# Two linear-attention blocks on one core: M's products spread over four token pairs, kv's products in two runs of three, and q's first loads given due times

## The chip, the core and the metric

The kernel runs on one core of a Trainium2 chip. The metric is the device time of one execution in microseconds. The core's engines work in parallel, each through its own queue in order: TensorE (PE; its weight loads are listed as PEld), VectorE (DVE), ScalarE (ACT), GpSimd (POOL) and SyncE (SP), which here only issues DMA transfers. An instruction that waits for a semaphore holds up everything behind it in its engine's queue.

## The reference

Two independent blocks, A and B, with inputs of their own; their results stand side by side. S = 2048 tokens, D = 640, 32 heads of 20.

```python
qkv = (x @ wqkv).reshape(B, S, 3, H, Dh)          # q, k, v
phi = lambda t: where(t > 0, t + 1, exp(t)) + 1e-6
pq, pk = phi(q), phi(k)
kv  = einsum("bhsd,bhse->bhde", pk, v)
z   = einsum("bhsd->bhd", pk)
num = einsum("bhqd,bhde->bhqe", pq, kv)
den = einsum("bhqd,bhd->bhq", pq, z) + 1e-6
return (num / den) @ wo                            # per block
```

## The kernel before, in words

All arithmetic is float32 made of pairs: a value is split into a high part (ACT rounds it, `hi_of`) and a low part (DVE subtracts, `lo_of`), and a product takes three matmuls. The value side is never formed per token. Instead G = x^T phi(k) is summed over tokens (`gstep`, tile psg, sums kept in gacc), kv = wv^T G per group of heads (`kvmm`, tile pskv, six groups of 6, 6, 6, 6, 4 and 4 heads, masked to the blocks of the heads), and M = kv wo (`mmm`, tile psm evacuated to mev, six groups too). M goes to memory (`md`), comes back (tile m), is turned into the nine sums that a Strassen-like product needs and into high and low parts (`forms("m", ...)` within `m_forms`), and those go to memory once more (fdh, fdl), from where the output stage loads them (fh, fl).

The first part of the kernel, some 290 us, handles k for both blocks. Tokens go through in pairs of tiles (`kpair(p, fill)`, 8 pairs a block, NPB = 8, NP = 16; pairs 0 to 2 take another path). A pair has seven steps of products (banks 0, 1 and 2 as tiles ka, ke, kb), each followed by evacuations on ACT and DVE (`copy`, `plus`) and by what `fill` puts there: gsteps of the group before, kv's products, M's products. Pairs 8 to 15 belong to block B; in them block A's kv and M are made. After pair 15 ten gsteps of the last group remain, and then the second part begins: the q stage, whose order is written out by hand (`at(slot, ...)`): products psq over 512 tokens, block B's own kv and M, the denominators and the output products (pa, pe, psb).

Order within the first part comes from a planner, run on the host while the program is built. Each job has an engine, an estimated cost, what it reads and writes, and optionally `ahead` (it may not be placed earlier than so many us before it is due), `late` (the due time of a job that nobody in the plan waits for, counted from `pe_at`, the sum of PE's costs so far, 25 by default), `due` (a fixed due time) and `safe` (a margin after a transfer). Due times are computed backwards from the readers. `emit` then walks forward in its own clock: each engine takes, of its jobs that are ready, the one due first, if tiles for it are free. A transfer costs wire time at 330 KB/us and is believed to have landed 1.9 us after that; its buffers are free from then on. PE's order is that of the calls. The chip then runs these orders against real semaphores.

Tiles come from slots: GD (31 of 640 columns), BD (7) and BO (4) are shared by nearly everything. The pool kx (for pairs) is closed by a planned job `gate`, and q1a and q1b (for q) open in its place. q's first loads are planned too: five pieces of wq (split into wh, wl), five of x (xqs, rounded to xqh), five low parts of x from memory (xql) and block B's wv.

z, the sum of phi(k) over tokens, is accumulated by transfers of GpSimd (`z_add`, zacc) and finished by `zsums`: DVE sums, transposes and reduces (zp), a store to memory (zd), four small loads (zq) and four small DVE steps (z, zs).

Of the kernel before, what the change touches and what calls it, by code (L numbers as in the profile page):

```python
# [15 lines left out]
DH = 20  # L16
EPS = 1e-6
GROUPS = [(0, 6), (6, 6), (12, 6), (18, 6), (24, 4), (28, 4)]
LAG = 0.2


class Space:
# [53 lines left out]
class Plan:  # L76
# [6 lines left out]
        self.jobs = []  # L83
        self.pe_at = 0.0

    def note(self, engine, n, fn, w, r, ahead=None, dma=None, late=None, by=None, due=None, safe=0.0):
# [22 lines left out]
        j.by, j.set, j.safe = by, due, safe  # L109
        self.jobs.append(j)  # L110
        return j

    def emit(self, start, log=None):
        jobs = self.jobs
        for j in reversed(jobs):
            due = min([n.due - LAG for n in j.nexts], default=j.late)
            if j.by is not None:
                due = min(due, j.late)
            due -= j.cost + (2.2 + j.dma if j.dma else 0)
            if j.engine == "PE":  # L120
                due = min(due, j.ideal)
            j.due = due if j.set is None else j.set
# [14 lines left out]
        while n < len(jobs):  # L137
# [7 lines left out]
            for e in idle:  # L145
# [46 lines left out]
                queue[e].remove(best)  # L192
                if best.dma:
                    wire = max(wire, now) + best.dma
                    best.done = wire + 1.9
                    if e == "SP":
                        flying.append(best.done)
                    idle[e] = now + best.cost
                else:
                    best.done = idle[e] = now + best.cost  # L200
                events.update((idle[e], best.done, best.done + LAG))
                ends.append((best.done, best))
                best.fn()
                if log is not None:
                    log.append((now, e, best.fn.__code__.co_firstlineno, best, best.done))
# [10 lines left out]
def tile_linear_attn_pair(ctx: ExitStack, tc: tile.TileContext, ins, out: bass.AP):  # L216
# [79 lines left out]

    BK = [Bank("bank", k) for k in range(8)]

    def load(dst, src, n, ahead=14.0, due=None):
        note("SP", 0.07, lambda: nc.sync.dma_start(dst.f, src), [dst], [], ahead=ahead, dma=n * 512 / 330e3, due=due)  # L300

    def hi_of(hi, src, n):
        note("ACT", n, lambda: act(hi.r, src.f, AF.Copy), [hi], [src], ahead=10.0)
# [51 lines left out]
    def forms(kind, src, split, ready=()):  # L355

        f, raw = {}, {}
        for c in range(NC):
            raw[c] = t = Space(kind, D, ANY)
            note("SP", 0.07, lambda t=t, c=c: nc.sync.dma_start(t.all.f, src[c * P:(c + 1) * P, :]), [t.all],  # L360
                 [mdv[0:6]] if kind == "m" else [], ahead=14.0, dma=1.0)
        for k in range(2):
            m, n = raw[k], raw[2 + k]
            x, z = Space("t23", D, ANY), Space("t4", HF, ANY)
            note("DVE", HF, lambda m=m, n=n, x=x: tt(x[HF:D].f, n[HF:D].f, m[HF:D].f, op=OP.subtract),
                 [x[HF:D]], [n[HF:D], m[HF:D]], ahead=10.0)
            note("DVE", HF, lambda m=m: tt(m[HF:D].f, m[HF:D].f, m[0:HF].f, op=OP.subtract),
                 [m[HF:D]], [m.all], ahead=10.0)
            note("DVE", HF, lambda m=m, n=n, x=x: tt(x[0:HF].f, n[HF:D].f, m[HF:D].f, op=OP.subtract),
                 [x[0:HF]], [n[HF:D], m[HF:D]], ahead=10.0)  # L370
            note("DVE", HF, lambda n=n, x=x, z=z: tt(z.all.f, n[0:HF].f, x[0:HF].f, op=OP.subtract),
                 [z.all], [n[0:HF], x[0:HF]], ahead=10.0)
            f[k], f[2 + k], f[4 + k], f[6 + k] = m, x, n, z
        x, m = Space("d5", HF, ANY), raw[4]
        note("DVE", HF, lambda: tt(x.all.f, m[0:HF].f, m[HF:D].f, op=OP.subtract), [x.all], [m.all], ahead=10.0)
# [211 lines left out]
    def zsums(b):  # L587

        z, zt32 = Space("zsum", D, ANY), Space("zturn", D, ANY)
        for h in range(2):  # L590
            note("DVE", HF, lambda h=h: tt(z.all.f[:, h * HF:h * HF + HF], zac[b][h].all.f[:, :HF],
                                           zac[b][h].all.f[:, HF:], op=OP.add), [z[h * HF:h * HF + HF]], [zac[b][h].all], safe=6.0)
        part, four = Space("zpart", 20), Space("zfour", 20)
        pt, ft4 = zp[b]
        add = dict(axis=mybir.AxisListType.X, op=OP.add)
        note("DVE", D, lambda: nc.vector.transpose(zt32.all.f, z.all.f), [zt32.all], [z.all])
        note("DVE", D, lambda: nc.vector.tensor_reduce(
            pt.rearrange("p (g c) -> p c g", g=4), zt32.all.f.rearrange("p (c g t) -> p c g t", g=4, t=32), **add),
            [part.all], [zt32.all])
        zdv = Space("zd", 1)  # L600
        note("SP", 0.07, lambda: nc.sync.dma_start(zd[b], pt), [zdv.all], [part.all], dma=0.1)
        for g in range(4):
            note("SP", 0.07, lambda g=g: nc.sync.dma_start(
                ft4[g * 32:g * 32 + 32].rearrange("p (q c) -> p q c", q=4),
                zd[b].rearrange("(q i) (g c) -> g i q c", q=4, g=4)[g]), [four[g:g + 1]], [zdv.all], dma=0.1, safe=6.0)
        zt, s = zz[b]

        def finish():
            nc.vector.tensor_reduce(zt, ft4.rearrange("p (q c) -> p c q", q=4), **add)
# [8 lines left out]
    def m_forms():  # L618
        def split(i, s):
            hi = Space("fsh", s.cols, ANY, F32R)  # L620
            lo = Space("fsl", s.cols, ANY, F32R)
            hi_of(hi.all, s.all, s.cols)
            lo_of(lo.all, s.all, hi.all, s.cols)
            fd[0, i] = [dram.tile([P, s.cols], F32, name=f"fd{t}0{i}") for t in "hl"]
            for d, t in zip(fd[0, i], (hi, lo)):
                note("SP", 0.07, lambda d=d, t=t: nc.sync.dma_start(d, t.all.f), [], [t.all], dma=s.cols / 640,
                     late=16.0 + 8.0 * (0, 2, 6, 4, 1, 3, 7, 5, 8, 9).index(i))

        forms("m", md[0], split)

# [161 lines left out]
    for c in range(NC):  # L792
        gstep(NG - 1, 0, c)
    wf[1] = forms("wk", ins[1]["wk"], w_split)
    kpair(NPB, filled(NG - 1, 1))
    kpair(NPB + 1, {0: [(kvmm, 0, 6)], 1: [(kvmm, 1, 7)], 2: [(kvmm, 2, 6)], 3: [(kvmm, 3, 7)],
                    4: [(kvmm, 4, 6), (kvmm, 5, 7)], 5: [(mmm, 0, 6)], 6: [(mmm, 1, 6)]})
    for p in range(NPB + 2, NP):
        i, h = divmod(p - NPB - 2, 2)
        gready(NG + i)  # L800
        fl = filled(NG + i, h, *((LAST,) if p == NP - 1 else ()))
        if p == NPB + 2:
            for n, g in ((0, 2), (2, 3), (4, 4), (6, 5)):
                fl.setdefault(n, []).append((mmm, g, 6))
        kpair(p, fl)
        if p == NPB + 2:
            zsums(0)
            m_forms()

    def swap():  # L810
# [28 lines left out]
    for c in range(NC):  # L839
# [8 lines left out]
            lo.make()  # L848
            tt(lo.all.r, raw.all.f, hi.all.f, op=OP.subtract)

        note("ACT", D, high, [hi.all], [raw.all, gate.all])
        note("DVE", D, low, [lo.all], [raw.all, hi.all])
        whl["q", 0, c] = hi, lo
    for c in range(NC):
        hi, lo, raw = late(q1b, "xqh", 512, 6), late(q1b, "xql", 512, 6), Space("xqs", 512, ANY)
# [7 lines left out]
            lo.make()  # L863
            nc.sync.dma_start(lo.all.f, xd[0][:, c].rearrange("p j s -> p (j s)"))

        note("ACT", 512, round, [hi.all], [raw.all, gate.all])
        note("SP", 0.07, fetch, [lo.all], [gate.all, xdv[0].all], ahead=30.0, dma=0.8)
        xt[0, c] = hi, lo
    for g, (h0, nh) in enumerate(GROUPS):
        cols = NC * DH * nh  # L870
        w = Space("wv", cols, (BD,))
        load(w.all, ins[1]["wv"][:, h0 * DH * NC:(h0 + nh) * DH * NC], cols, 30.0)
        w.left += 1
        wvt[1, g] = w
    plan.emit(1.0, globals().get("LOG"))
# [515 lines left out]
```

## Time and profile before

| | |
|---|---|
| median of 3 runs | 572.95 us (572.63 to 574.16) |
| profiled execution | 574.53 us, span 572.8 us from first to last instruction |
| PE busy | 565.7 us of the span |
| DVE, ACT, POOL busy | 434.3, 341.4, 57.2 us |
| granted clock of PE | 0.999 |
| DMA | 117.64 MB, mean 205 GB/s |
| chain that ended last | PE 89%, DMA 5%, DVE 3% |

A row of the order of time reads: start and duration in us, engine, line, operation, output and inputs, tile sizes, how many were merged (x), and in brackets how long the engine stood idle before it and what ended that. Matmuls are pipelined, so one lasts 0.31 us by its row while the next starts 0.15 us after it. A row of the waits reads: who waited, for whom, us in total, times, the longest. In the table by stages each stretch has its length, then busy time with the number of instructions for PE, PEld, DVE, ACT and POOL, the granted clock, the DMA share and GB/s. A row of transfers reads: out and in, queue, count, KB each, median us from issue to landing.

### The profile page before, as it was taken

What the parts mean: (1) busy time and instruction counts of PE and PEld (TensorE: products, weight loads), DVE (VectorE), ACT (ScalarE), POOL (GpSimd) and SP (SyncE); (2) the same over time, 40 slices, a digit from 0 to 9 for tenths busy, and PEclk for the clock granted to TensorE, in tenths of its full rate; (3) what the DMA queues carried; (4) which work ended last, traced back from release to release, by engine and by line L of the source; (5) the groups of instructions that cost most, each with busy time, mean ns of one, the idle gap of its engine ahead of it and who ended that gap; (6) DMA issues with size and microseconds to landing.
All of it is one profiled execution on the core that took longest, in us unless ns stands there. A gap on an engine that the chain in (4) does not pass through costs nothing.

```text
span 572.8 us, 9505 instructions
## 1 busy us (share of the span) xinstructions
PE 565.7 (99%) x3524; PEld 535.8 (94%) x3524; DVE 434.3 (76%) x706; ACT 341.4 (60%) x619; POOL 57.2 (10%) x93
## 2 busy tenths in 40 slices
PE   8999999999999999999999999999999999999997
PEld 6999999999999999999988899898989989898997
DVE  6788687599888589976555699967788786758792
ACT  6877566673786677655156665646556464644551
POOL 0210011110010011100000103120012201001010
PEclk9999999999999999999999999999999999999999
DMA  8994665758858889786787986663363996122022
GB/s 296 379 242 141 163 183 128 205 143 246 278 144 217 250 249 321 216 252 196 211 245 275 339 276 215 226 218 109 120 225 134 355 390 231 47 76 93 0 93 92
DMA packets 69441, 117.64 MB, mean 205 GB/s; under 512 B 7956, under 2 KB 31252, under 8 KB 69396
## 3 DMA queue, kind: packets, MB, share of 16 engines
q1 hardware_dynamic: 60500, 89.98, 48.2%
q0 software_dynamic: 8608, 26.88, 16.7%
q8 instruction: 27, 0.44, 0.3%
q10 hardware_dynamic: 288, 0.20, 0.1%
q14 instruction: 18, 0.15, 0.1%
HBM read 71.13 MB, written 35.41 MB: 186 GB/s over the span
## 4 chain that ended last, share of the span: by engine, by line
PE 89%; DMA 5%; DVE 3%; ACT 1%; issue 1%; SPq 1%; ACTq 0%; DVEq 0%
PE psg L312 20%; PE pa L1191 12%; PE ka L312 8%; PE psq L912 8%; PE psq L914 8%; PE psq L913 8%; PE pe L1191 6%; PE ke L312 4%; PE psk L711 4%; PE psb L1191 4%; PE kb L312 3%; DMA md<-mev 2%; DMA wk<-in_A_wk 1%; PE pskv L551 1%; PE pskv L972 1%; DMA xqs<-in_A_xt 1%
## 5 line engine op out<-in xcount | busy, mean ns | idle before, releaser
L312 PE MATMUL psg<-pkl,xnh 128*128 128x320 f32 x320 | 98.9, 309 | 0.0
L312 PE MATMUL psg<-pkh,xnh 128*128 128x320 f32 x320 | 98.8, 309 | 0.0
L312 PE MATMUL psg<-pkh,xnl 128*128 128x320 f32 x320 | 98.4, 308 | 0.0
L912 PE MATMUL psq<-xqh,wh 128*128 128x512 f32 x200 | 78.6, 393 | 1.0 <-ACT xqh L860 1.0
L914 PE MATMUL psq<-xqh,wl 128*128 128x512 f32 x200 | 78.0, 390 | 0.0
L913 PE MATMUL psq<-xql,wh 128*128 128x512 f32 x200 | 77.9, 390 | 0.0
L312 PEld LDWEIGHTS psg<-pkl,xnh 128*128 128x128 f32 x320 | 60.1, 188 | 0.0
L312 PEld LDWEIGHTS psg<-pkh,xnl 128*128 128x128 f32 x320 | 60.1, 188 | 0.0
L312 PEld LDWEIGHTS psg<-pkh,xnh 128*128 128x128 f32 x320 | 60.0, 188 | 0.0
L1206 ACT ACTIVATE o<-pa 128x320 f32<-128x320 f32 x64 | 27.9, 438 | 45.2 <-PE pa L1191 45.0
L484 ACT ACTIVATE kt<-ka 128x320 f32<-128x320 f32 x52 | 22.6, 435 | 52.2 <-PE ka L312 49.0
L1082 DVE SCALAR_TENSOR_TENSOR pq<-eq,rq 128x512 f32<-128x512 f32 x40 | 27.6, 691 | 30.7 <-ACT rq L1081 30.6
L401 POOL DMA_DIRECT2D zacc<-ek x32 | 26.4, 836 | 244.5 <-DVE ek L494 185.3
L532 DVE TENSOR_TENSOR gacc<-psg,gacc 128x320 f32<-128x320 f32 x60 | 29.4, 489 | 28.1 <-PE psg L312 27.3
L1080 ACT ACTIVATE eq<-psq 128x512 f32<-128x512 f32 x40 | 23.9, 597 | 36.6 <-PE psq L914 34.2
L912 PEld LDWEIGHTS psq<-xqh,wh 128*128 128x128 f32 x200 | 37.6, 188 | 8.5 <-ACT xqh L860 1.3
L914 PEld LDWEIGHTS psq<-xqh,wl 128*128 128x128 f32 x200 | 37.5, 188 | 7.9
L913 PEld LDWEIGHTS psq<-xql,wh 128*128 128x128 f32 x200 | 37.6, 188 | 7.2
L396 ACT ACTIVATE pkh<-ek,epst 128x640 fp32r<-128x640 f32 x32 | 26.5, 829 | 7.9 <-DVE ek L494 7.5
L1191 PE MATMUL pa<-fh,dah 128*128 128x320 f32 x96 | 29.7, 309 | 0.0
L1191 PE MATMUL pa<-fh,dal 128*128 128x320 f32 x96 | 29.7, 309 | 0.0
L1191 PE MATMUL pa<-fl,dah 128*128 128x320 f32 x96 | 29.7, 309 | 0.0
(213 smaller groups left out, 1553.3 us busy)
## 6 DMA issues: line engine op xcount, KB each, us to landing
zacc<-ek POOLq DMA_DIRECT2D x32, 320.0 KB, 5.8
xql<-xd SPq DMA_DIRECT2D x40, 256.0 KB, 5.9
xd<-xl SPq DMA_DIRECT2D x29, 320.0 KB, 6.2
out<-o POOLq DMA_DIRECT2D x28, 320.0 KB, 3.6
xns<-in_A_x SPq DMA_DIRECT2D x16, 320.0 KB, 5.8
xts<-in_B_xt_tiles SPq DMA_DIRECT2D x16, 320.0 KB, 4.3
xns<-in_B_x SPq DMA_DIRECT2D x16, 320.0 KB, 5.1
xqs<-in_A_xt SPq DMA_DIRECT2D x20, 256.0 KB, 6.0
```

Of the source, the lines that this page charges most:

```text
L312: nc.tensor.matmul(o, a.r, w.r, start=start and k == i == 0, stop=k == n - 1 and i == 2, skip_group_check=True)
L396: note("ACT", n + 110, lambda: act(hi.r, p.f, AF.Identity, bias=epst), [hi], [p, K0.all], by=8.0)
L401: note("POOL", 1.0, lambda: nc.gpsimd.dma_start(z.f, p.f, **kw), [z], [p], dma=1.0 if first else 1.86)
L532: tt(o, BK[k].tile[:, :HF], o, op=OP.add)
L711: nc.tensor.matmul(o[h][:, :HF], x[a].r, w[c][h * HF:h * HF + HF].r, start=c == 0 and i == 0, stop=c == NC - 1 and i == 2, skip_group_chec ...
L912: nc.tensor.matmul(o, whi, xhi, start=first, stop=False)
L913: nc.tensor.matmul(o, whi, xlo, start=False, stop=False)
L914: nc.tensor.matmul(o, wlo, xhi, start=False, stop=last)
L1080: nc.scalar.activation(e, ps, AF.Exp)
L1082: nc.vector.scalar_tensor_tensor(pq[u][:, c, :], e, 1.0, r, op0=OP.min, op1=OP.add)
L1191: nc.tensor.matmul(ps, x, y, start=start and n == i == 0, stop=n == len(terms) - 1 and i == 2, skip_group_check=True)
L1206: copy = lambda x, y: nc.scalar.activation(x, y, AF.Copy)
```

## The change

1. The planner: a transfer is believed to have landed `lat` after the wire, 3.0 us (LAT) instead of 1.9, unless it has a fixed due time; a transfer's buffers count as taken for 6 us (REUSE) after that. Due times of transfers move earlier by the same 1.1 us.
2. kv's products of block A, one after each of steps 0 to 3 and two after step 4 of pair 9, become two runs of three, after steps 1 and 4.
3. M's products: two in pair 9 and four in pair 10 become one in pair 9 (step 5), two in pair 10 (steps 0 and 2), two in pair 11 (steps 0 and 2), one in pair 12 (step 0). Pair 10's gsteps take the later places (LAST).
4. `zsums(0)` follows pair 12 and `m_forms()` pair 13; both followed pair 10. The stores of M's forms get closer due times, and the differences of M's rows a margin (`safe`) of 6 us.
5. The z store and its four loads are issued by GpSimd instead of SyncE, for both blocks.
6. q's first jobs get due times of their own: splits of wq 9 us after the end of PE's planned work instead of 25, rounding of x 8, low parts of x 6 to 10, wv 10 to 20; `ahead` is smaller for the low parts and wv.

```diff
+LAT = 3.0
+REUSE = 6.0
 ...
+        j.by, j.set, j.safe, j.lat = by, due, safe, (LAT if due is None else 1.9) + lat
 ...
-            due -= j.cost + (2.2 + j.dma if j.dma else 0)
+            due -= j.cost + (j.lat + 0.3 + j.dma if j.dma else 0)
 ...
-                    best.done = wire + 1.9
+                    best.done = wire + best.lat
 ...
-                events.update((idle[e], best.done, best.done + LAG))
-                ends.append((best.done, best))
+                free = best.done + (REUSE if best.dma else 0.0)
+                events.update((idle[e], best.done, best.done + LAG, free))
+                ends.append((free, best))
 ...
     def forms(kind, src, split, ready=()):
+        safe = 6.0 if kind == "m" else 0.0
 ...
-        note("SP", 0.07, lambda: nc.sync.dma_start(zd[b], pt), [zdv.all], [part.all], dma=0.1)
+        note("POOL", 1.0, lambda: nc.gpsimd.dma_start(zd[b], pt), [zdv.all], [part.all], dma=0.1, lat=2.0)
         for g in range(4):
-            note("SP", 0.07, lambda g=g: nc.sync.dma_start(
+            note("POOL", 1.0, lambda g=g: nc.gpsimd.dma_start(
 ...
-                     late=16.0 + 8.0 * (0, 2, 6, 4, 1, 3, 7, 5, 8, 9).index(i))
+                     late=10.0 + 5.5 * (0, 2, 6, 4, 1, 3, 7, 5, 8, 9).index(i))
 ...
-    kpair(NPB + 1, {0: [(kvmm, 0, 6)], 1: [(kvmm, 1, 7)], 2: [(kvmm, 2, 6)], 3: [(kvmm, 3, 7)],
-                    4: [(kvmm, 4, 6), (kvmm, 5, 7)], 5: [(mmm, 0, 6)], 6: [(mmm, 1, 6)]})
-    for p in range(NPB + 2, NP):
-        i, h = divmod(p - NPB - 2, 2)
-        gready(NG + i)
-        fl = filled(NG + i, h, *((LAST,) if p == NP - 1 else ()))
-        if p == NPB + 2:
-            for n, g in ((0, 2), (2, 3), (4, 4), (6, 5)):
-                fl.setdefault(n, []).append((mmm, g, 6))
+    place = ((1, 5, 0, 6), (2, 0, 1, 6), (2, 2, 2, 6), (3, 0, 3, 6), (3, 2, 4, 6), (4, 0, 5, 6))
+    kvs = {1: [(kvmm, g, (6, 7, 3)[g]) for g in range(3)], 4: [(kvmm, g, (4, 5, 6)[g - 3]) for g in range(3, 6)]}
+    for p in range(NPB + 1, NP):
+        if p == NPB + 1:
+            fl = kvs
+        else:
+            i, h = divmod(p - NPB - 2, 2)
+            gready(NG + i)
+            fl = filled(NG + i, h, *((LAST,) if p in (NPB + 2, NP - 1) else ()))
+        for q, n, g, k in place:
+            if q == p - NPB:
+                fl.setdefault(n, []).append((mmm, g, k))
         kpair(p, fl)
-        if p == NPB + 2:
+        if p == NPB + 4:
             zsums(0)
+        if p == NPB + 5:
             m_forms()
 ...
-        note("ACT", D, high, [hi.all], [raw.all, gate.all])
-        note("DVE", D, low, [lo.all], [raw.all, hi.all])
+        note("ACT", D, high, [hi.all], [raw.all, gate.all], ahead=15.0, late=9.0)
+        note("DVE", D, low, [lo.all], [raw.all, hi.all], ahead=15.0, late=9.0)
 ...
-        note("ACT", 512, round, [hi.all], [raw.all, gate.all])
-        note("SP", 0.07, fetch, [lo.all], [gate.all, xdv[0].all], ahead=30.0, dma=0.8)
+        note("ACT", 512, round, [hi.all], [raw.all, gate.all], late=8.0)
+        note("SP", 0.07, fetch, [lo.all], [gate.all, xdv[0].all], ahead=12.0, dma=0.8, late=6.0 + c)
 ...
-        load(w.all, ins[1]["wv"][:, h0 * DH * NC:(h0 + nh) * DH * NC], cols, 30.0)
+        load(w.all, ins[1]["wv"][:, h0 * DH * NC:(h0 + nh) * DH * NC], cols, 14.0, late=10.0 + 2 * g)
```

More of the change, by code (lines that the diff above doesn't have):

```diff
@@ L84, in __init__, with note @@
         self.pe_at = 0.0
-    def note(self, engine, n, fn, w, r, ahead=None, dma=None, late=None, by=None, due=None, safe=0.0):
+    def note(self, engine, n, fn, w, r, ahead=None, dma=None, late=None, by=None, due=None, safe=0.0, lat=0.0):
         base = self.RATE.get(engine)
@@ L297, in tile_linear_attn_pair, with load @@
     BK = [Bank("bank", k) for k in range(8)]
-    def load(dst, src, n, ahead=14.0, due=None):
-        note("SP", 0.07, lambda: nc.sync.dma_start(dst.f, src), [dst], [], ahead=ahead, dma=n * 512 / 330e3, due=due)
+    def load(dst, src, n, ahead=14.0, due=None, late=None):
+        note("SP", 0.07, lambda: nc.sync.dma_start(dst.f, src), [dst], [], ahead=ahead, dma=n * 512 / 330e3, due=due,
+             late=late)
     def hi_of(hi, src, n):
@@ L365, in forms @@
             note("DVE", HF, lambda m=m, n=n, x=x: tt(x[HF:D].f, n[HF:D].f, m[HF:D].f, op=OP.subtract),
-                 [x[HF:D]], [n[HF:D], m[HF:D]], ahead=10.0)
+                 [x[HF:D]], [n[HF:D], m[HF:D]], ahead=10.0, safe=safe)
             note("DVE", HF, lambda m=m: tt(m[HF:D].f, m[HF:D].f, m[0:HF].f, op=OP.subtract),
-                 [m[HF:D]], [m.all], ahead=10.0)
+                 [m[HF:D]], [m.all], ahead=10.0, safe=safe)
             note("DVE", HF, lambda m=m, n=n, x=x: tt(x[0:HF].f, n[HF:D].f, m[HF:D].f, op=OP.subtract),
-                 [x[0:HF]], [n[HF:D], m[HF:D]], ahead=10.0)
+                 [x[0:HF]], [n[HF:D], m[HF:D]], ahead=10.0, safe=safe)
             note("DVE", HF, lambda n=n, x=x, z=z: tt(z.all.f, n[0:HF].f, x[0:HF].f, op=OP.subtract),
-                 [z.all], [n[0:HF], x[0:HF]], ahead=10.0)
+                 [z.all], [n[0:HF], x[0:HF]], ahead=10.0, safe=safe)
             f[k], f[2 + k], f[4 + k], f[6 + k] = m, x, n, z
         x, m = Space("d5", HF, ANY), raw[4]
-        note("DVE", HF, lambda: tt(x.all.f, m[0:HF].f, m[HF:D].f, op=OP.subtract), [x.all], [m.all], ahead=10.0)
+        note("DVE", HF, lambda: tt(x.all.f, m[0:HF].f, m[HF:D].f, op=OP.subtract), [x.all], [m.all], ahead=10.0, safe=safe)
         f[8], f[9] = m, x
```

1 line of the change is left out of this document (removed).

## The prediction

> **What bounds the kernel now.** I read the page's totals first, then the waits of TensorE (PE), then PE's own order of time around each wait, then SyncE's (SP's) order before the worst one.
>
> ```profile
> span 572.8 us, 9505 instructions
> PE 565.7 (99%) x3524; PEld 535.8 (94%) x3524; DVE 434.3 (76%) x706; ACT 341.4 (60%) x619; POOL 57.2 (10%) x93
> ...
> PE psq L912 <- ACT xqh L860: 1.0, 1, 1.0
> ...
> PE ke L312 <- DVE kt L488: 0.7, 1, 0.7
> ```
>
> PE is busy 565.7 of 572.8 us and the change leaves its 3524 matmuls as they are. A rearrangement can only move PE's holes. The other waits of that view belong to the first ten microseconds, whose loads keep their fixed due times, but for one of 0.2 us. What a neighbouring matmul's end covers does not show there, so I looked at start times. Matmuls of 320 columns start 0.147 us apart; these pairs are further apart:
>
> ```profile
> 165.49 0.30 PE L578 MATMUL psm<-woh,kvl 120*120 120x320 f32 x1
> 165.76 0.41 PE L578 MATMUL psm<-woh,kvh 120*120 120x320 f32 x1
> ...
> 179.31 0.31 PE L578 MATMUL psm<-woh,kvl 80*80 80x320 f32 x1
> 179.87 0.42 PE L312 MATMUL ka<-wkh,xh 128*128 128x320 f32 x1 [0.25 <-ACT kt L484]
> ...
> 200.49 0.31 PE L312 MATMUL psg<-pkh,xnl 128*128 128x320 f32 x1
> 200.80 0.41 PE L312 MATMUL ke<-wkh,xsh 128*128 128x320 f32 x1
> ...
> 204.71 0.31 PE L312 MATMUL ka<-wkh,xl 128*128 128x320 f32 x1
> 205.74 0.41 PE L312 MATMUL ke<-wkh,xsh 128*128 128x320 f32 x1 [0.71 <-DVE kt L488]
> 205.99 0.31 PE L312 MATMUL ke<-wkl,xsh 128*128 128x320 f32 x1
> ...
> 289.29 0.31 PE L312 MATMUL psg<-pkh,xnl 128*128 128x320 f32 x1
> 290.61 0.50 PE L912 MATMUL psq<-xqh,wh 128*128 128x512 f32 x1 [1.02 <-ACT xqh L860]
> ```
>
> Start to start less 0.147, plus the slow restart behind each (205.74 to 205.99 is 0.25, so 0.10 more): 0.27 - 0.147 + 0.10 = 0.22; 0.56 - 0.147 + 0.10 = 0.51; 0.31 - 0.147 + 0.10 = 0.26; 1.03 - 0.147 + 0.10 = 0.98; 1.32 - 0.147 + 0.10 = 1.27. Together 3.25 us, all between 165 and 291 us, which is the stretch that the change rearranges. That is what can be had: 0.57% of the span.
>
> **The change part by part.**
>
> *M's products and what follows them.* Before, the six products (psm, six matmuls each) lie in pairs 9 and 10; zsums(0) and m_forms follow pair 10. After, one is in pair 9, two in 10, two in 11, one in 12; zsums(0) follows pair 12 and m_forms pair 13. The matmul count is the same, 36 of 0.147 us, so the cost is in who waits. What is removed is a vector engine (DVE) that was full and stood behind a transfer:
>
> ```profile
> 200.00:234.00 34.00, 33.28 (x226) 32.75 (x225) 31.63 (x61) 24.05 (x42) 3.41 (x4) 1.00 0.95 285
> 234.00:289.30 55.30, 55.30 (x380) 55.30 (x378) 37.01 (x66) 27.89 (x45) 5.15 (x6) 1.00 0.75 215
> ...
> DVE t L365 <- issue: 3.7, 1, 3.7
> ...
> 205.20 0.48 DVE L488 TENSOR_TENSOR kt<-ke,kt 128x320 f32<-128x320 f32 x1
> L306 DVE TENSOR_TENSOR fsl<-m,fsh x5: 812/816/825, 200.7 to 249.6; 128x640 fp32r<-128x640 f32 x5
> ```
>
> In the stage table the fourth number group is DVE: busy 31.63 of 34.00 us between 200 and 234. The first difference of M (L365) stood 3.7 us for M's rows to come back from memory, and everything in DVE's queue stood with it, the evacuation L488 at 205.20 included, for which PE waits at 205.74. After the change M's last rows leave in pair 12, near 206 us, and are read back after pair 13, near 234, so nothing stands. That takes the holes at 200.80 and 205.74 (0.26 + 0.98). The holes at 165.76 and 179.87 (0.22 + 0.51) lie at two products of M in one pair, each waiting for ScalarE (ACT) to empty the bank; one product where two were takes most of this.
>
> Where it goes: M's forms are nine half-width differences and ten splits, on DVE 9 x 0.48 + 7 x 0.82 + 3 x 0.48 = 11.5 us (0.48 for half width as L488, 0.82 for full width as L306), into a stretch where DVE was busy 37.01 of 55.30. Two thirds of the splits' stretch, 200.7 to 249.6, lay before 234, so some 7.7 us come on top: 44.7 of 55.3, or 81%, less than the 93% before. The slack of DVE hides them; without it, at 93%, they cost holes like the two above.
>
> The cover that it thins: kv's products in two runs leave steps 2 and 3 of pair 9 without filling, so bank 0's copy has one step of nine matmuls (1.32 us) to hide behind where a filled pair gives twelve more (1.76). Bounds: 0 (ACT idle) and 0.51 us, the hole at 179.87, which is a copy of bank 0 come late, at each of two places (here, and at the products in steps 0 and 2 of pair 10). I take 0.3 in all, nearer the low end, since two holes in six products is what the denser order showed.
>
> *kv's products in two runs of three.*
>
> ```profile
> 151.75 1.05 PE pskv L551 x10
> ...
> 160.35 1.43 PE pskv L551 x20
> ```
>
> A group of 120 columns costs 1.05 us alone; the two of 80 that already stand together cost 1.43, that is 0.72 each. A break costs nothing that I can see beyond one slow restart of 0.08 to 0.10. Five breaks become two: gain between 0 and 0.3, I take 0.1.
>
> *q's first loads.* This is the largest hole, and SP's order shows it:
>
> ```profile
> 267.63 2.23 SPq L864 DMA_DIRECT2D xql<-xd  x5
> ...
> 275.47 8.44 SPq L300 DMA_DIRECT2D wq<-in_A_wq  x5
> 284.01 0.38 SPq L601 DMA_DIRECT2D zd<-zp  x1
> 284.43 5.02 SPq L300 DMA_DIRECT2D xqs<-in_A_xt  x5
> ...
> DMA to landing us min/median/max: 5.7/6.1/7.0
> L860 ACT ACTIVATE xqh<-xqs x5: 630/631/635, 289.9 to 292.9; 128x512 fp32r<-128x512 f32 x5
> ...
> SPq L300 <- DMA zacc<-ek: 33.8, 8, 11.3
> ```
>
> The five wq loads take 8.44 us to leave, the five xqs loads wait behind them and behind the z store, and the first xqs leaves 5 us before PE is through. By the planner's constants a wq load could go from 25 - 0.82 - 0.2 - 0.72 - 0.2 - 0.07 - 3.19 = 19.8, less its `ahead` of 20, so 0.2 us before the planned end of PE; with late=9 and the new latency it is due at 2.7 and may go 17.3 us before that end. xqs goes from 1.1 after to 17.0 before. xql's `ahead` falls from 30 to 12 and wv's from 30 to 14, so the ten loads that PE needs pass the eleven that it needs later or can have late. REUSE=6 keeps the planner from handing a load the buffer of an accumulating store that is still in flight (the 33.8 us row, eight waits). The lines on landing and on L860 are those of the tile xqs. The five xqh need 5 x 0.63 = 3.2 us on ACT, which has slack there (27.89 of 55.30). I let the whole 1.27 go, and 0.2 stay for the turn from one kind of product to the other.
>
> *The z transfers move from SP's queue to POOL's.* The store waits for DVE's reduction, the four loads for the store, and on POOL the next z accumulation or M store queues behind them. For input A the queue behind is the accumulation of pair 13, whose issuer is 10% busy. For input B only M's second stores follow, in q's part. But DVE's last planned step reads these loads, and q's first kv evacuations stand behind it:
>
> ```profile
> 283.00 0.81 DVE L597 TENSOR_REDUCE zp<-zturn 128x20 f32<-128x640 f32 x1
> 293.60 0.19 DVE L609 TENSOR_REDUCE z<-zq 128x5 f32<-128x20 f32 x1 [1.16 <-DMA zq<-zd]
> 294.29 0.27 DVE L976 TENSOR_TENSOR kvt<-pskv,mask 120x120 f32<-120x120 f32 x1
> ...
> 297.00 0.26 PE L972 MATMUL pskv<-gacc,wv 128*120 128x120 f32 x1
> ...
> fdh<-fsh SPq DMA_DIRECT2D x7, 320.0 KB, 3.4
> fdh<-fsh POOLq DMA_DIRECT2D x7, 320.0 KB, 2.5
> ...
> zd<-zp SPq DMA_DIRECT2D x2, 10.0 KB, 5.3
> DMA to landing us min/median/max: 2.9/3.6/4.4
> L401 POOL DMA_DIRECT2D zacc<-ek x32: 547/854/1194, 19.5 to 271.8; - x32
> ```
>
> The third kv product (297.00) takes the first one's bank, so it needs the evacuation at 294.29; with PE 1.3 earlier it comes at 295.7. The trace has no small transfer on POOL. The nearest rows: POOL's issues (0.55 to 0.85), its 320 KB store (2.5 to landing), SP's small ones (store 5.3, loads 2.9 to 4.4, the landing line of the tile zq). Low end: 283.8 + 2.5 + 3 x 0.55 + 2.9 = 290.9, no stall. High end: the plan puts the sums 1.1 later, so 284.9 + 5.3 + 3 x 0.85 + 4.4 = 297.2, and 1.0 us for z's steps and the evacuation (293.60 to 294.56): 298.2, a stall of 2.5. The middle, 284.4 + 3.9 + 2.1 + 3.6 = 294.0, ends at 295.0, ahead of 295.7; I take 0.3.
>
> [...]
>
> *LAT, REUSE and safe everywhere.* The planner's belief in a load's landing goes from 1.9 to 3.0 us past the wire, and buffers of transfers stay taken 6 us longer, so orders on SP, ACT and DVE shift from 10 us on, where PE has no hole to lose. Below: no gain, there is none to take. Above: one new hole of the size of the old ones, 1.0. I take 0.3.
>
> **Sum.** 3.25 + 0.1 - 0.3 - 0.2 - 0.3 - 0.3 = 2.25 us off. Behind 291 us PE waits for nothing, so all of it arrives at the end. The profiled execution took 574.53 for its span of 572.8 (1.7 around it), which gives 572.3; it was 1.6 above the median of the runs shown, 572.95 (572.63 to 574.16). On the median: 570.7.
>
> **The rivals.**
>
> *Only q's start is mended, the rest returns elsewhere.* Spread M products still meet a backlogged ACT, the new order brings holes of 0.5 to 1.0: gain 1.27 - 0.2 plus little, 0 to 1.6, time 571.3 to 573. For it: DVE at 93% shows how little it takes. Against it: the load is levelled, not added.
>
> *The edit on q's loads does nothing.* They are placed early but find no free buffer, since M's forms now hold theirs at the same time (two splits every 5.5 us, each 6 us longer). Then the 1.27 stays and the gain is 1.0: 572.0. This lies within the first rival's range and I count it there.
>
> *Slower: M's stores now stand in front of q's loads.*
>
> ```profile
> SPq L626 <- ACT fsh L303: 15.3, 7, 8.5
> ...
> 217.00:234.00 17.00, 17.00 (x119) 17.00 (x118) 16.19 (x30) 12.06 (x20) 1.71 (x2) 1.00 0.98 314
> ```
>
> All twenty stores now leave after 234, among q's 21 transfers, and SP waits in order, up to 8.5 us for one split. Traffic is no limit: the forms' loads and stores (5 x 320 + 14 x 320 + 6 x 160 KB, 7.2 MB, two thirds of it new here) add 4.8 MB in 55.3 us, 215 + 87 = 302 GB/s, and 314 was carried between 217 and 234 with PE busy 17.00 of 17.00. The order is: the last xqs must leave by 289.3 - 7.0 - 3.2 = 279. It may leave from 272. One wait of 8.5 loses 1.5 us of what was won. Two such waits put it at 289, as before, or past it; from 5 us past the old 289.1 on, the kernel is slower by over 0.3%. Two waits plus the 5.0 us that the xqs took to leave give 294, some 575.
>
> **How the numbers follow.** 0.3% (1.7 us) is about what a measurement of this kernel can tell from no change. Forecast, 569.3 to 571.2: 0.56. Partly mended, 571.3 to 574.6, from little gained to the z stall's high end on top: 0.32. Slower: 0.12, with the planner's reordering in it. The range runs from all holes gone and the kv joins at 0.3 (572.95 - 3.55 = 569.4) to 573.8, which leaves out the slow cases and a little of the partial ones.
>
> **What would show it.** PE's holes at 200 and 205 gone, with DVE below 85% busy between 200 and 234; all xqs issued before 280 and xqh done before PE's last psg; psq following psg within 0.3 us; pskv as two blocks of about 3.1 and 2.5 us; zq landed before 295 and no wait at the third kv product of q. Wrong would be: a first psq still waiting on xqh, PE holes over 0.5 us in pairs 9 to 15, or DVE's z step ending past 296.

## The result: 1.5% slower, and the profile after

| | before | after |
|---|---|---|
| median | 572.79 us (571.95 to 576.57, 6 runs) | 582.25 us (581.27 to 583.24, 6 runs) |
| profiled execution, span | 574.53, 572.8 | 582.17, 580.4 |
| granted clock of PE | 0.999 | 0.991 |

The ratio is 1.0152, 95% interval 1.0123 to 1.0182: 9.5 us slower, where 2.2 faster was forecast. The time lies outside the range and on the other side. The half of the change that I had worked out in detail did what it should. The loss is in the item that I had put at 0.3 us: block B's z transfers.

The page's totals of the changed kernel, then its waits of PE (who waited, for whom: us in total, times, the longest):

```profile
span 580.4 us, 9491 instructions
PE 567.1 (98%) x3524; PEld 538.1 (93%) x3524; DVE 434.1 (75%) x706; ACT 341.7 (59%) x619; POOL 63.1 (11%) x103
```

```profile
PE pskv L981 <- DVE kvt L985: 8.0, 1, 8.0
PE psi L644 <- DVE ones L324: 1.0, 1, 1.0
PE pskv L981 <- DVE gacc L537: 0.7, 1, 0.7
```

The waits for xqh and kt are gone, and one of 8.0 us is new: the third kv product of q waits for the evacuation that frees its bank. PE's order of time shows the two ends of the stretch that matters:

```profile
286.89 0.31 PE L316 MATMUL psg<-pkh,xnl 128*128 128x320 f32 x1
287.04 0.40 PE L921 MATMUL psq<-xqh,wh 128*128 128x512 f32 x1
...
288.61 1.28 PE L981 MATMUL pskv<-gacc,wv 128*120 128x120 f32 x10 [0.71 <-DVE gacc L537]
...
302.44 2.35 PE L981 MATMUL pskv<-gacc,wv 128*120 128x120 f32 x10 [8.01 <-DVE kvt L985]
```

The last psg starts 2.40 us earlier than before (286.89 against 289.29), and the first psq 3.57 earlier (287.04 against 290.61). So at the start of q's part the change was 3.6 us ahead. Then, start to start and less the usual distance, the first kv product adds 0.88, the third 8.19, and the matmuls behind it run slowly for another 2.2. That is -3.57 + 0.88 + 0.07 (a restart) + 8.19 + 2.22 = +7.8, against 580.4 - 572.8 = 7.6 between the spans. The stage table (length, busy time of PE, PEld, DVE, ACT and POOL, granted clock, DMA share, GB/s) shows both halves:

```profile
200.00:234.00 34.00, 34.00 (x234) 34.00 (x233) 25.01 (x48) 20.59 (x36) 5.77 (x8) 1.00 0.65 176
234.00:286.90 52.90, 52.90 (x363) 52.90 (x362) 43.01 (x77) 32.25 (x52) 5.11 (x6) 1.00 0.92 285
...
292.00:296.00 4.00, 2.43 (x16) 1.81 (x14) 0.00 (x0) 0.00 (x0) 2.23 (x4) 1.00 0.98 293
...
296.90:307.00 10.10, 4.56 (x16) 4.08 (x17) 2.88 (x11) 3.08 (x7) 0.00 (x0) 0.50 0.52 119
307.10:320.00 12.90, 12.90 (x81) 11.22 (x80) 6.71 (x13) 6.41 (x16) 1.25 (x2) 1.00 0.68 221
```

Up to 286.9 PE is full; DVE, 31.63 of 34.00 before, is at 25.01. From 292 to 296 DVE and ACT do nothing at all while the DMA engines are at 0.98. Between 296.9 and 307.0 PE is granted half its clock (0.50; psq's matmuls start 0.43 us apart there, 0.23 behind it), and that costs the 2.2 us after the stall. What DVE waits for is the z loads, as its own order says, with POOL's beside it:

```profile
285.89 0.48 DVE L596 TENSOR_TENSOR zsum<-zacc 128x320 f32<-128x320 f32 x1
...
287.29 0.82 DVE L602 TENSOR_REDUCE zp<-zturn 128x20 f32<-128x640 f32 x1
...
301.42 0.19 DVE L614 TENSOR_REDUCE z<-zq 128x5 f32<-128x20 f32 x1 [12.92 <-DMA zq<-zd]
...
302.11 0.27 DVE L985 TENSOR_TENSOR kvt<-pskv,mask 120x120 f32<-120x120 f32 x1
```

```profile
288.40 0.58 POOL L606 DMA_DIRECT2D zd<-zp  x1 [17.64 <-DVE zp L602]
292.72 2.23 POOL L608 DMA_DIRECT2D zq<-zd  x4 [3.74 <-DMA zd<-zp]
```

The store leaves at 288.40 and lands 4.0 us later. The loads leave from 292.72 to 294.40, and the last lands at 301.34, 6.9 us after its issue. The first kv evacuation of q, L985, stands behind z's step in DVE's queue, though it needs nothing of z.

### The profile page after: what moved, and what is told of

Same layout as the page of the kernel before. It is cut to its first block, busy times and chain, and to the rows that moved or that the text cites. A ratio compares the mean times of both kernels' runs of the same rounds, so it can differ in the third digit from the quotient of the medians.

```text
span 580.4 us, 9491 instructions
## 1 busy us (share of the span) xinstructions
PE 567.1 (98%) x3524; PEld 538.1 (93%) x3524; DVE 434.1 (75%) x706; ACT 341.7 (59%) x619; POOL 63.1 (11%) x103
## 4 chain that ended last, share of the span: by engine, by line
PE 96%; DMA 2%; DVE 1%; POOL 0%; issue 0%; DVEq 0%
PE psg L316 24%; PE pa L1200 12%; PE ka L316 10%; PE psq L922 8%; PE psq L921 8%; PE psq L923 8%; PE pe L1200 6%; PE ke L316 5%; PE psk L716 4%; PE psb L1200 4%; PE kb L316 3%; DMA zq<-zd 1%; PE pskv L556 1%; PE psm L583 1%; PE pskv L981 1%; PE psi L644 1%
```

## The experiments

Theories. A: the loss is z's lateness alone, because DVE executes z's step ahead of q's first evacuation. B: q's early loads or M's stores cost by themselves. If A, the next question is why z is late: its issuer (GpSimd), its late start, or the traffic around it. "Hole" means start to start in PE's order less the usual distance; ratios are to the kernel before on the same chip, with their 95% interval.

### z_later: the same transfers, nobody behind them

Block B's z steps are taken out of the plan and placed by hand among q's later steps; the transfers are untouched.

```diff
-        note("DVE", 300, finish, [KZ[b].all], [four.all], safe=6.0)
+        if b == 0:
+            note("DVE", 300, finish, [KZ[b].all], [four.all], safe=6.0)
+        else:
+            zlast.append(finish)
...
+    at(("q", 1, 0, 3), zlast[0])
```

> The changed kernel with one edit: block B's four small z steps on VectorE leave the plan and stand in q's order in the second group of 512 tokens (z of B is wanted only four groups later). Theory 1 (the whole loss is the 8.2 us hole at q's third kv product, because those steps wait for the z loads in VectorE's queue in front of kv's evacuations, and the 2.2 us of matmuls at half clock behind the hole): both go, 10.4 us off the changed kernel, about 571.8, at or a little under the kernel before, granted clock 1.00 throughout; the 0.9 us hole at q's first kv product stays. Rival (something else in q's start is late too, the late wv or xql loads, and the z steps only hide it): another hole of several us appears at the second to fourth kv product or at psq, time 574 to 580.

Measured: 572.69 us, ratio 0.9991 (0.9979 to 1.0004). The z loads are no faster, 7.3 us at worst, but nobody waits for them. The slow stretch is gone too (clock 0.999). PE's waits:

```profile
PE pskv L986 <- DMA wv<-in_B_wv: 1.2, 1, 1.2
PE psi L649 <- DVE ones L324: 1.0, 1, 1.0
PE pa L1205 <- ACT o L1220: 0.4, 1, 0.4
```

So A holds: moving four small vector steps gives back the loss. What remains is a first kv product that waits for wv, a hole of 1.33 us, and a new one of 0.54 at 338.

### z_on_sync: block B's z transfers back on SyncE

```diff
-        note("POOL", 1.0, lambda: nc.gpsimd.dma_start(zd[b], pt), ...)
+        note(zq, zc, lambda: ze.dma_start(zd[b], pt), ...)   # SP for b == 1; the four loads too
```

> The changed kernel with block B's z store and its four loads back on SyncE (block A's stay on GpSimd). Theory 2 (GpSimd's path is what makes the z loads take 7 us): with SyncE's 2.6 to 3.8 us a hop as in the kernel before, z arrives about 288.5 + 4 + 1.5 + 3 = 297, hole 8.2 -> 4, time 576 to 577. Theory 3 (the later place of VectorE's z sums, and the traffic of wv and wo loads at 288 to 300, are what makes it late, the issuer is nothing): the loads queue behind the same traffic, z at 300 to 302, the hole stays 7 to 9 us, 581 to 583; and SyncE stands still for the reduction, so wv and wo leave later.

Measured: 574.57 us, ratio 1.0027 (1.0008 to 1.0045). The hole shrinks from 8.19 to 2.21 us, and the clock stays at 1.00 in the profile. That is less than either theory had given (576 to 583 us). The loads leave at the same time as in the changed kernel (292.83 to 294.15) and land in 1.6 to 1.8 us. The stage table shows one reason:

```profile
292.00:296.00 4.00, 2.96 (x19) 2.27 (x17) 0.01 (x1) 0.00 (x0) 0.00 (x0) 1.00 0.32 55
```

The DMA engines are at 0.32, not 0.98. While SP stands at the z loads, waiting for the store, nothing behind them leaves: the first wo load goes at 294.68, where the changed kernel starts them at 289.50. So two things changed here, issuer and traffic, and this run doesn't tell them apart.

### z_early: the sums two microseconds sooner

```diff
-        ..., [zac[b][h].all], safe=6.0)
+        ..., [zac[b][h].all], safe=0.0 if b else 6.0)
```

> The changed kernel with no margin (safe=0) on block B's two z sums: they, the transpose and the reduction stand two evacuations earlier in VectorE's queue, as in the kernel before; the loads stay on GpSimd. If the later place of the sums is what counts (theory 3): the reduction ends 3.5 us earlier, the store and loads with it, hole 8.2 -> about 4 or less, the 0.9 us hole at q's first kv product goes, clock loss shrinks, 574 to 577. If the loads wait for the traffic whatever their start (they land when wv and wo are through): landing stays near 300, 580 to 582.

Measured: 580.64 us, ratio 1.0132 (1.0115 to 1.0149). The store leaves at 286.43, 2.0 us sooner, and the last load lands at 299.88, 1.5 sooner, still 6.7 us after its issue; the hole is 5.88. So two microseconds of the start are worth 2.3 us of the hole. The second sum stands 4.7 us later than before the change, and no run of the changed kernel puts it back all the way, so what the whole of its lateness costs is not shown.

### before_z_pool: only item 5, on the kernel before

The planner's extra 2.0 us of latency for the store (`lat`) is left out.

```diff
-        note("SP", 0.07, lambda: nc.sync.dma_start(zd[b], pt), ...)
+        note("POOL", 1.0, lambda: nc.gpsimd.dma_start(zd[b], pt), ...)   # the four loads too
```

> The kernel before with only the z store and loads of both blocks moved from SyncE to GpSimd. If GpSimd's path alone makes z late (theory 2): store at 283.9, loads leave at 288 instead of 289.5 and take 7 instead of 2.6 us, z at 295 to 297, a hole of 0 to 1.5 us at q's third kv product, 573 to 575. If not: SyncE no longer stands for the reduction, xqs may leave earlier, same time or up to 1 us faster, 572 to 573.

Measured: 574.74 us, ratio 1.0018 (1.0000 to 1.0037). The loads, on GpSimd, land 2.0 to 3.2 us after their issue, and there is no hole at the third kv product. In this kernel the wo loads still leave late, at 292.38, and the DMA share from 292 to 296 is 0.69:

```profile
292.00:296.00 4.00, 4.00 (x29) 3.60 (x28) 1.49 (x7) 1.92 (x4) 0.24 (x1) 1.00 0.69 194
```

So GpSimd as issuer doesn't make z late by itself, in this traffic. The hole at the first psq is 0.6 us longer than before (1.81 against 1.17), against the hope that SP, freed of z, would send x sooner.

### wo_behind_z: same issuer, less traffic ahead

The six wo loads go to GpSimd's queue, behind the z loads.

```diff
-        nc.sync.dma_start(o, ins[b]["wo"][h0 * DH:(h0 + nh) * DH, :])
+        nc.gpsimd.dma_start(o, ins[b]["wo"][h0 * DH:(h0 + nh) * DH, :])
```

> The changed kernel with block B's six wo loads (1.6 MB) issued by GpSimd, behind its four z loads, instead of by SyncE ahead of them; z stays on GpSimd. If traffic ahead of the z loads is what delays them: landing 3 to 5 us instead of 7, z about 297.5 to 299, hole 4 to 6 us, 576 to 579. If GpSimd's path is slow by itself: 7 us, no change, 581 to 583 (wo later costs nothing while the hole is there).

Measured: 577.51 us, ratio 1.0072 (1.0045 to 1.0099). Issued by the same engine at the same time (292.44 to 294.10), the loads now land in 2.9 to 3.7 us where it was 6.9 to 7.1, and the hole is 3.96.

```profile
292.00:296.00 4.00, 2.35 (x16) 1.74 (x14) 0.00 (x0) 0.00 (x0) 3.56 (x7) 1.00 0.65 172
...
299.20:302.40 3.20, 3.20 (x10) 2.56 (x9) 1.33 (x4) 2.44 (x6) 0.00 (x0) 0.50 1.00 231
```

With the issuer and the moment kept, less traffic (DMA share 0.65 against 0.98 from 292 to 296) halves the loads' time. A hole of 3.96 us already brings a stretch of half clock, 3.41 us long by the clock record.

### z_on_scalar: a third issuer under nearly the same traffic

Block B's z transfers are issued by ScalarE; the wo loads leave between 289.39 and 295.9. The page of the kernel before lists ACT's queue with the kind of SP's: `q10 hardware_dynamic`, 0.20 MB (the two loads that ACT issues there), and `q1 hardware_dynamic`, 89.98 MB; GpSimd's is `q0 software_dynamic`, 26.88 MB.

```diff
-        note("POOL", 1.0, lambda: nc.gpsimd.dma_start(zd[b], pt), ...)
+        note(zq, zc, lambda: ze.dma_start(zd[b], pt), ...)   # ACT for b == 1; the four loads too
```

> The changed kernel with block B's z store and loads issued by ScalarE: a queue of its own, of the same kind as SyncE's, while SyncE goes on with its loads. SyncE's version brought the hole from 8.2 to 2.2 us, its small loads landing in 2.5 instead of 7 us, but SyncE also stood still for the z store and held back six wo and four xqs loads. If GpSimd's way of issuing is slow: the loads land in 2 to 3 us here too, hole 2 to 4 us, 574 to 576. If it is the traffic let loose by SyncE not standing: they take 6 to 7 us here as on GpSimd, hole 7 to 9 us, 580 to 582.

Measured: 579.44 us, ratio 1.0094 (1.0067 to 1.0122). The first load lands 4.1 and the last 4.7 us after its issue, the hole is 4.83.

```profile
292.00:296.00 4.00, 2.38 (x16) 1.77 (x14) 0.00 (x0) 0.00 (x0) 0.00 (x0) 1.00 0.95 249
...
298.60:301.90 3.30, 2.86 (x12) 2.76 (x13) 1.73 (x7) 1.58 (x4) 0.00 (x0) 0.50 0.79 251
```

This lies between the two theories: with the DMA engines nearly full (0.95) it is worse than wo_behind_z with 0.65, and better than GpSimd with 0.98. It is not quite an exchange of issuers alone, since the six wo loads, 3.4 us from first to last in the changed kernel, take 6.8 us to leave here. All kernels side by side, with DMA share and GB/s from the first issue of block B's four z loads to the last landing (a share can come out a little over 1 in this view; I read it as full):

| kernel | issuer | DMA share, GB/s meanwhile | z loads, issue to landing |
|---|---|---|---|
| q_due (below) | SP | 0.11, 4 | 1.7 us |
| z_on_sync | SP | 0.23, 21 | 1.6 to 1.8 |
| before_z_pool | POOL | 0.57, 165 | 2.0 to 3.2 |
| before | SP | 0.66, 183 | 2.9 |
| wo_behind_z | POOL | 0.67, 171 | 2.9 to 3.7 |
| z_on_scalar | ACT | 0.96, 237 | 4.1 to 4.7 |
| m_spread (below) | SP | 1.02, 326 | 4.8 to 5.4 |
| after | POOL | 1.00, 254 | 6.9 to 7.1 |
| z_early | POOL | 1.03, 268 | 6.7 to 7.0 |
| z_later and its three variants, filler | POOL | 1.00 to 1.05, 245 to 280 | 6.8 to 7.9 |

Where the share is moderate, no issuer stands out: at 0.57 to 0.67 GpSimd's 2.0 to 3.7 us are the level of SP's 2.9. At a full share one does: GpSimd's loads took 6.7 to 7.9 us in seven kernels, SP's 4.8 to 5.4 with more GB/s around them, and ACT's 4.1 to 4.7. That points to an issuer's part of some 1 to 4 us, an estimate from these rows (6.7 - 5.4 to 7.9 - 4.1). No run changes the issuer with the same transfers ahead, so its size stays open.

### filler: the same hole, filled with matmuls

34 matmuls of no use, 512 columns each, stand ahead of q's third kv product; they add work where PE stood idle.

```diff
+        if g == 2:
+            fill = bank("psf", "a", 2)
+            for _ in range(34):
+                nc.tensor.matmul(fill, same, same.unsqueeze(1).to_broadcast([P, 4, P]), start=True, stop=True)
```

> The changed kernel with 34 more matmuls on TensorE (constant tile, 512 columns, into a bank that nobody reads then) in front of q's third kv product: some 34 x 0.227 = 7.7 us of work into the hole of 8.2 us. If the slow matmuls behind the hole (2.2 us, granted clock 0.50) come from TensorE having idled: no slow stretch, granted clock 1.00 all along, about 2.2 us under the changed kernel, near 580.0. Rival (they are slow from something else, the DMA or the banks at that place): the stretch stays slow, 582.

Measured: 581.87 us, ratio 1.0151 (1.0117 to 1.0184). In the trace the slow stretch is gone (clock 1.00 from 302.4 to 307.0, where it was 0.50), and the profiled execution took 580.41 with a span of 578.6, 1.8 less. But its runs spread from 580.41 to 583.46 (granted clock 1.00 in three of the four), and the median is not resolved from the changed kernel's. That the half clock here came of PE's idling is shown (0.50 behind the hole, 1.00 with the hole filled); that filling it saves the 2.2 us is not.

### m_spread: only M, kv and what follows them, on the kernel before

Items 2, 3 and 4, without the margin of M's rows; the z transfers on SP, q's due times as they were. The diff is those parts of the change's.

> The kernel before with only the products of M spread, kv's runs of three, and zsums(0) and m_forms moved (with the stores' closer due times); planner constants, z on SyncE and q's due times as before. My prediction's terms for this part were 0.22 + 0.51 + 0.26 + 0.98 us of holes gone, less 0.3. In SyncE's order the z store now comes ahead of the five wq loads, so they wait for VectorE's reduction (283.8 before, 282 with the holes gone). If that counts: the holes between 165 and 206 go (2 us), the hole at the first psq grows from 1.3 to 3 to 5 us, sum 573 to 576. If SyncE catches up: 571.5 to 572.

Measured: 578.85 us, ratio 1.0090 (1.0067 to 1.0113). PE's holes at 165, 179, 200 and 205 are gone, with one of 0.45 at 196 in their place. The loss, more than the 573 to 576 us that I had expected at worst, is at q's start. First SP's order of time, then the waits of SP's queue between 240 and 290 us:

```profile
284.09 0.33 SPq L601 DMA_DIRECT2D zd<-zp  x1
...
286.83 3.31 SPq L300 DMA_DIRECT2D xqs<-in_A_xt  x5
```

```profile
SPq L626 <- ACT fsh L303: 12.5, 5, 6.3
SPq L626 <- DVE fsl L306: 8.5, 6, 2.2
...
SPq L601 <- DVE zp L597: 0.9, 1, 0.9
```

The wq loads leave between the z store and the xqs, from 284.51 on, where they left from 275.47 before: SP stands 21 us for splits of M that it is to store, and last for zp. What that does to ACT's order, to PE's waits and to the clock (stage table):

```profile
289.88 3.10 ACT L849 ACTIVATE wh<-wq 128x640 fp32r<-128x640 f32 x4 [1.23 <-DMA wq<-in_A_wq]
292.89 2.53 ACT L864 ACTIVATE xqh<-xqs 128x512 fp32r<-128x512 f32 x4
```

```profile
PE psq L916 <- ACT xqh L864: 5.5, 1, 5.5
```

```profile
290.50:297.20 6.70, 3.65 (x14) 3.35 (x15) 3.56 (x7) 5.35 (x9) 0.00 (x0) 0.50 1.03 319
```

The rounding of x stands behind that of wq on ACT, so late wq loads make late xqh. This is my third rival, M's stores in front of q's loads; its price is a hole of 5.63 us and a slow stretch. In the whole change it doesn't happen, and it doesn't in z_later_oldlat and z_on_sync either, which undo items 1 and 5 (for block B): that leaves q's due times as what prevents it.

### q_due: only q's due times, on the kernel before

```diff
-        note("ACT", D, high, [hi.all], [raw.all, gate.all])
+        note("ACT", D, high, [hi.all], [raw.all, gate.all], ahead=15.0, late=9.0)
...
```

The rest of item 6 likewise; all else is the kernel before.

> The kernel before with only q's due times (item 6), z on SyncE. My prediction gave 1.27 - 0.2 us for it. The ten loads that q needs first leave first, wv behind them, the z store and loads last on SyncE. Holes between 165 and 206 stay (2 us); the hole at the first psq goes; a hole of up to 1.3 us at the first kv product for wv and up to 1 at the third for z may open: 572.5 to 574.5, no difference that can be measured.

Measured: 573.49 us, ratio 1.0009 (0.9991 to 1.0028). The hole at the first psq is gone (psg at 287.85, psq at 288.00), and those at 179 and 204 are there (0.39 and 0.58). A new one of 0.83 appears at the first kv product, as in the changed kernel.

```profile
PE pskv L973 <- DVE gacc L533: 0.7, 1, 0.7
```

The last xqs leave at 267.4. z's second sum moves from 281.24 to 286.85, one place ahead of the last evacuation of gacc, and the store to 289.09. SP stands 8.1 us for it, the DMA engines are at 0.01 from 286 to 290, the four loads land in 1.7 us, and z's step is done by 294.6; there is no hole at the third kv product. The gain at psq is given back at the next step, and the time shows no change.

### z_later_oldlat: LAT and REUSE undone

z_later with the planner's old belief.

```diff
-LAT = 3.0
-REUSE = 6.0
+LAT = 1.9
+REUSE = 0.0
```

> z_later (572.7, 0.9991 of the kernel before) with the planner's old belief (LAT 1.9, REUSE 0). If LAT and REUSE are what keeps the first part free of holes (no matmul started late between 10 and 287 us in the changed kernel): holes of 0.2 to 1 us come back, 573 to 575. If they do nothing there: within 0.5 us of z_later.

Measured: 575.46 us, ratio 1.0033 (1.0012 to 1.0055). No hole returns before 287. The wv loads leave later, and the first kv product waits 2.4 us for them, a hole of 2.58 without any slow stretch in the profiled execution. So item 1 is not what removes the holes in the middle; it moves the wv loads forward.

### z_later_wv and z_later_wv2: what the runs point to

z_later with wv due sooner and the z sums without their margin; in the second, z's steps are placed one stage later still, at `("q", 2, 2, 3)`.

```diff
-        load(w.all, ins[1]["wv"][...], cols, 14.0, late=10.0 + 2 * g)
+        load(w.all, ins[1]["wv"][...], cols, 20.0, late=4.0 + 3 * g)
```

> The changed kernel with block B's z steps out of the plan (as in z_later), block B's wv loads due 4 to 19 us after TensorE's planned end instead of 10 to 20 with ahead 20 (the first of them passes the last xqs), and no margin on the z sums. z_later kept a hole of 1.3 us at q's first kv product, waiting for wv. That goes: 1.3 under z_later, about 571.4, 0.4% under the kernel before. Rival: wv in front pushes xqs and xql back and opens as long a hole at the first psq: same as z_later, 572.7.

> z_later_wv (571.6, 0.996) with the four z steps one group of tokens later still, since a hole of 0.5 us at 337 us (an output product waiting for ScalarE) stands only in the two kernels where those steps lie in q's second group. If they make it: 0.5 less, 571.1. If not: the same, 571.6, with the hole still there.

Measured: 571.61 us, ratio 0.9960 (0.9942 to 0.9977), and 571.35 us, ratio 0.9960 (0.9945 to 0.9975). In the first the hole at the first kv product is gone and one of 0.53 at 338 stays; in the second that one is gone too, and PE's waits are those of the first microseconds alone:

```profile
PE psi L650 <- DVE ones L324: 1.0, 1, 1.0
PE psk L722 <- ACT wkh L307: 0.4, 1, 0.4
```

Both beat the kernel before, by 0.4%, and the changed one; between the two no difference is resolved. By the medians the last is 1.7 us under the kernel before (571.35 against 573.04): what the change could give with z and wv out of the way.

## Why the prediction was wrong, point by point

**M's products.** Right. All four holes are gone, as m_spread shows for this part alone; z_later_oldlat shows that it isn't LAT and REUSE. DVE, which I had put at 81% behind 234 us, is busy 43.01 of 52.90 there, 81%. The thinned cover (0.3) cost nothing in the changed kernel; in m_spread one hole of 0.45 appeared.

**kv in two runs (0.1).** Nothing, as far as it can be read. In the chain of work the blocks took 3.15 and 2.48:

```profile
152.18 3.15 PE pskv L556 x30
...
158.85 2.48 PE pskv L556 x30
```

Together 5.63, and before 4 x 1.05 + 1.43 = 5.63.

**q's first loads (1.27 - 0.2).** Right in place and size: psq follows psg after 0.15 us. The last xqs left at 280.56, half a microsecond past the 280 that I had asked for, which did no harm. I had not priced what else item 6 does. wv, with `ahead` 14 and a late due time, leaves between 283.6 and 289.4, and z's second sum stands ahead of the last evacuation of gacc. The first kv product has a hole of 0.8 to 1.3 us in the changed kernel, z_later and q_due: it ends with gacc in the changed kernel and q_due, and with wv in z_later, by the rows of the waits above.

**LAT and REUSE (0.3).** No hole came of them; in the one pair of profiles that shows it they helped at wv, by 1.25 us (2.58 less 1.33).

**The z transfers (0.3, high end 2.5).** This is the step that failed, and its high end with it: 284.9 + 5.3 + 3 x 0.85 + 4.4 = 297.2, against 301.34. Term by term, with the difference to that sum:

- The reduction ended at 288.11, not 284.9: +3.2. The second z sum stood at 285.89 instead of 281.24, one place ahead of the last evacuation of gacc; I had moved it by the 1.1 us of LAT only. Item 6 does this by itself, and POOL's larger costs in the planner don't: the rows below are of the kernel before, of before_z_pool (item 5 alone) and of q_due (item 6 alone, z on SP), and in z_on_sync, with block B's transfers planned on SP, the sum stays late, at 286.33. That the splits of wq, due sooner, take DVE's places ahead of the sum fits the order (all five before it in q_due, all behind it in the kernel before), but no run moves them alone.

```profile
281.24 0.48 DVE L591 TENSOR_TENSOR zsum<-zacc 128x320 f32<-128x320 f32 x1
```

```profile
281.15 0.48 DVE L591 TENSOR_TENSOR zsum<-zacc 128x320 f32<-128x320 f32 x1
```

```profile
286.85 0.48 DVE L592 TENSOR_TENSOR zsum<-zacc 128x320 f32<-128x320 f32 x1
```

- The store took 4.0 where the sum had 5.3 (the middle of two stores of 3.8 and 6.8), and the issues 1.7 where the sum had 2.6: together -1.6 with the gaps between the steps.
- The loads took 6.9 to 7.1 where I had 4.4 at most: +2.5. That bound came from loads on SP's queue (block A's; block B's took 2.9). In the kernel before, the wo loads stood behind z's in SP's queue and went at 291.85, after them. With z off SP alone (before_z_pool) they go no sooner, at 292.38: by the profile SP waits 5.2 us there for the xqs loads. In the changed kernel q's loads are earlier too, and the wo loads go at 289.50, ahead of z. My bound was taken from rows under a condition that the change itself removes.

Neither item does harm at the third kv product alone: before_z_pool has item 5 and q_due has item 6, and neither has a hole there. The changed kernel has both, a late store and nothing that holds the bulk loads back for it. I had priced the items one by one and had no term for the pair. That it is the pair fits these runs, but none has the two without the other items.

With PE 1.4 sooner than I had it (the bank was wanted at 294.26, not 295.7), a stall of 2.5 became 8.2. Then came a term that I had nowhere, 2.2 us of half clock behind the stall.

I had named the mechanism, DVE's z step ahead of the kv evacuations, and its check ("DVE's z step ending past 296": its last row ended at 302.19). I should have made it the slower rival. That rival was instead M's stores in front of q's loads, which m_spread shows to be real, and which item 6 keeps from happening.

**The sum.** Up to the first psq I had -2.55 (all but z's 0.3) and the spans show -3.57. But the holes were read from one execution of 574.53, 1.6 above the median, and its runs spread from 571.1 to 577.5. By the medians the best version gains 1.7 where the spans differ by 3.6 (572.8 against 569.2). So part of what looked like holes to be had belongs to a slower execution than the median.

## What to carry to other kernels

When a waiting transfer is moved off a queue, ask what stood behind it there: that traffic may now go first (here the wo loads, at 289.50 instead of 291.85), and the moved transfer's latency is then no longer the one in the trace (6.9 to 7.1 us instead of 2.9). Price parts of a change that touch one path together: here the later store and the freed queue cost at most 0.4% each alone, by the intervals of q_due and before_z_pool, and 8 us of stall came where both were there. An in-order engine should not have a step that needs a round trip through memory ahead of work that others wait for; placing z's four small steps later gave back 9 us here, while making the trip faster gave back 3 to 8. And a stall of PE should be priced with the half clock that may follow it: here 0.50 for 3.41 to 10.24 us, behind holes of 3.96 to 8.19 us.

## What the runs showed of the hardware

The time of z's small loads (2.5 KB each) from issue to landing rose with the DMA share meanwhile. On SP's queue it was 1.6 to 1.8 us at 0.11 to 0.23 and 4.8 to 5.4 at 1.02; on GpSimd's 2.0 to 3.7 at 0.57 to 0.67 and 6.7 to 7.9 at 1.00 to 1.05.

PE's granted clock fell to 0.50 after a stall, and to nothing in between. By the clock records of the traces the slow stretches lasted 10.24 us (after), 6.83 (z_early, m_spread), 3.42 (z_on_scalar) and 3.41 (wo_behind_z). They followed holes of 8.19, 5.88, 5.63, 4.83 and 3.96 us; holes of 2.21 (z_on_sync) and 2.58 (z_later_oldlat) brought none in the profiled executions. That sets no firm threshold: three of z_on_sync's seven runs, whose holes are not on record, have a mean clock of 0.997, as wo_behind_z's profile has with its one slow stretch, and took 1.1 to 1.7 us longer than the profiled one; of z_later_oldlat's ten runs seven have 0.997 and one 0.994. In the changed kernel the slow stretch began at 296.81, 2.5 us after PE ran out of work, and ended at 307.05, 4.6 us after it had work again.

The five lengths are within 0.02 us of one, two or three times 3.41 us; what sets that length is not shown.
